# Two-stage set attention and SwiGLU on one core: order of the first stages, wait of GpSimd for VectorE's integer steps, 64-column unread products, new lists

## The chip, the cores and the metric

The kernel runs on one core of a Trainium2 chip. The metric is the device time of one launch in microseconds (us), the median of several runs. The engines of the core are TensorE (PE; its weight loads are shown as PEld), VectorE (DVE), ScalarE (ACT) and GpSimd (POOL); each works through its own instructions in the order in which the program issues them. Transfers are issued by the sync queue (SP).

## The reference

x has 4 batches of 12,416 rows of 128 channels, `inducing` 32 rows. Per batch there are two attentions without projections, then a gated feed-forward layer over all 49,664 rows with d_ff = 1,536:

```python
def mab(q, kv):
    s = scale * (q @ kv.transpose(0, 2, 1))
    s = s - s.max(-1, keepdims=True)
    a = np.exp(s)
    a /= a.sum(-1, keepdims=True) + 1e-09
    return a @ kv
h = mab(I, x)
x2 = mab(x, h)                                  # (B, N, C), then (B*N, C)
rms = np.sqrt(np.mean(x2 * x2, axis=-1, keepdims=True) + 1e-06)
xn = x2 / rms * rms_g
g = xn @ w_gate
out = (g / (1.0 + np.exp(-g)) * (xn @ w_val)) @ w_out
```

The three weight matrices reach the kernel as 64-bit floats.

## The kernel before, in words

**Algebra.** The rows of x2 are weights `a` (32 numbers a row) times h. The kernel normalizes `a` itself and multiplies it with `h @ w_gate` and `h @ w_val` ("stacks" `sg` and `sv`), so that a gate product has only the 32 weights in two halves (high and low part, each twice: 128 rows) as its moving side.

**Tiling.** A batch is cut into 7 sets of rows (`NS`), these into 25 units of up to 512 rows; with 12 column blocks of d_ff there are 4 x 25 x 12 = 1,200 blocks. Each has a gate product (`gate`, L709), SiLU (L719), a value product (`value`, L737), their multiply (`times_value`, L751) and the product with `w_out`. The last comes in three kinds, given by the list `sorts`: P is one plain 32-bit product (in two instructions, L807), S and D are three products in a faster 32-bit form (L795, L796, L807) of a high and a low part. S makes the parts with ACT (L764) and DVE (L770) and adds them with POOL (L815); D with ACT (L761, L783) and POOL (L777, L815).

**Order by hand.** The order of everything is written out in lists of letters. `ORDER` is that of the first stages (batch 0 up to its first two units), `program` that of the rest; each letter issues one step, and a "." in `program` takes the next number of `taken`, a step outside the blocks (attention of the next batch, norms, the other weights). `banks` and `BANKS` tell which of the 8 PSUM banks each product writes to, `workers`, `outputs`, `holders` and `picks` which buffer a step uses and which of the waiting blocks it takes.

**The first stages.** Names of `ORDER` that matter here, with s a set, k a part, i a weight matrix (0 gate, 1 value, 2 out) and c one of its three chunks of 512 columns or rows; a last letter A, V or G names the engine (ACT, DVE, POOL):

- `t`sk, `c`sk: PE turns four tiles of x (L934), a copy out of PSUM (L919 on ACT, L923 on DVE)
- `s`, `m`, `own`, `mB`, `nb`, `e`, `r`, `h`: scores of a set (PE, L316), their eviction with a maximum (DVE, L945), the maximum of a group of sets (L951, L959, L962), exponentials (ACT, L970), transpose (DVE, L354), sum with x (PE, L978). `ls`, `share`, `shared`, `tl`, `spl`, `rl`, `fr`, `hs`, `th` bring the groups together, `hT` copies the turned h (ACT, L919), `hg` scales it.
- `p`ic, `u`ic, `g`ic, `l`ic: a weight's 64-bit word taken apart on DVE: exponent (`power`, L231), upper mantissa (`upper`, L244), sign (`sign`, L253), lower mantissa (`lower`, L259). These are the integer steps. `P` and `U` turn two of them into numbers (L209, L211, L213); `j`ic multiplies the two on POOL (`join`, L265); `q` stores the chunk and fetches the next.
- `sc`, `T`, `rm`, `sub`, `ex`, `ta`, `sq`, `zm`, `sm`, `mm`, `rt`, `ap`, `tb`, `hi`, `lo`, for parts 0, 1, 2 of set 0: scores against h (PE, L1025), transpose (DVE, L1028), row maximum (DVE, L1032) and its subtraction (L1036), exponential (ACT, L1041), transpose (DVE, L1045), product with the Gram matrix of h (PE, L1049), its multiply and sum (DVE, L1053, L1058), clamp (L1062), power -1/2 (POOL, L1066), multiply (L1070), transpose (DVE, L1073), high and low part (L1078, L1084).
- `st`i, `stc`i, `low`i: the first third of a stack (PE, L479; ACT, L482; DVE, L486). It needs `j`i0.
- `sdh`, `sdl`, `sdm`, `cpa`, `cpb` for units 0 and 1: selection products that spread the halves over 128 rows (PE, L1088) and their copies to the gate product's moving side.
- `w`n: n products of the identity with itself into bank 5, which nobody reads (`warm`, L158); 7 stand at the start of the kernel as well. Each is a 32-bit product in two instructions with a weight load each.
- `silu`: a first SiLU, with its table load (ACT, L1107).

In the `program` part a step of the kinds `power`, `upper`, `sign`, `lower` makes the next POOL instruction wait for it; this is a dependency made by hand, with the reason "no two at the shared port". `ORDER` is gone through without it (`for name in ORDER.split(): do[name]()`).

Of the kernel before, what the change touches and what calls it, by code (L numbers as in the profile page):

```python
# [18 lines left out]
P = 128  # L19
# [4 lines left out]
def kernel(  # L24
# [10 lines left out]
    nc = tc.nc  # L35
# [119 lines left out]
    def warm(n):  # L155
        ps = pall[:, 5, :]
        for _ in range(n):
            nc.tensor.matmul(ps[:, 0:P], ident[:], ident[:], start=True, stop=True)  # L158
# [113 lines left out]
    turns, works, outs, factors = [], [], [], []  # L272

# [600 lines left out]
    for s in (1, 2, 0, *range(3, NS)):  # L874
# [20 lines left out]
        sdm0 silu tb1 hi1 cpb0A p01 cpa0V lo1V P01A w1 sdh1 sdm1 sdl1 cpb1A cpa1A u01 U01V  # L895
# [6 lines left out]
    def first():  # L902
# [217 lines left out]
        for n in range(1, 40):  # L1120
            do[f"w{n}"] = lambda n=n: warm(n)
# [124 lines left out]
    def seams():  # L1246
# [13 lines left out]
        5672340156372450721456701425140571240715420745127450172407512510752317052317024537032407263742746043267304234073  # L1260
        4270327053127305127031251512450126401526140526041245143624532757364735263456735745146517507654107641754055172457
        3571725742135724130725412354615267526471260541072467043764162106714625014725437240732413072103271403716207365127
        6351726513267136364716376471630714306217420761405726450145102614264350264032520754302434750324102475146506267467
        0526470357620165073126507261576507610576501463154634165462526531246534127651675042607456270452706534253761374623
        4726314672312470612764125714257162517462714751467104360146703476014721367306327652062763765230176501201327041270
        2731047230276346734267432643572453670524605246104561462105640216412354362514516521467562317546230152304624254302
        4675204375230170412032731243710421013641263416536253421632451637167457614164501765124705140512521054314523045301
        2754207356047235275204352407310723420473407624073062753046705435637306350160576132751037501347531740537415074316
# [290 lines left out]
```

## Time and profile before

| | |
|---|---|
| median of 3 runs | 1476.39 us (1476.35 to 1476.93) |
| profiled execution | 1473.84 us, of it the span 1472.1 |
| PE, DVE, ACT, POOL busy | 99%, 97%, 89%, 93% of the span |
| mean granted TensorE clock | 0.999 |
| x of batch 0 | 6.4 MB, in five loads of 1 MB and some smaller ones |

The span goes from the first to the last instruction. A row of the timeline or of the costliest groups has the engine, the source line, the operation, what it writes and reads, shapes, the count, and in brackets the idle time before it with what ended it. In a timeline a row begins with start and duration in us, and instructions of one kind in a row are merged (x2, x3). In the chain of waits a row has start, duration and the engine and line that the end depended on. A matmul's end is modelled.

### The profile page before, as it was taken

The numbers are of one execution on the slowest core, as the hardware profiler recorded it, in microseconds if no ns is written. First come the engines' busy times: TensorE is split into PE (matmuls) and PEld (weight loads), VectorE is DVE, ScalarE is ACT, GpSimd is POOL, SyncE is SP. The second block draws the span as 40 slices with busy tenths as digits, with TensorE's granted clock in tenths as the row PEclk, the third lists the DMA queues.
The fourth block names the chain that finished last, engine by engine and source line by source line (L and its number), as shares of the span: only waits on it lengthen the run. The fifth ranks groups of instructions, "written<-read, shape, count | busy, mean of one in ns | idle before, by whom it ended". The sixth has DMA issues, their size and how long they took to land.

```text
span 1472.1 us, 26044 instructions
## 1 busy us (share of the span) xinstructions
PE 1462.6 (99%) x7303; PEld 1105.9 (75%) x7303; DVE 1427.8 (97%) x2483; ACT 1305.7 (89%) x2604; POOL 1374.5 (93%) x1212
## 2 busy tenths in 40 slices
PE   9999999999999999999999999999999999999998
PEld 7566777867777777786777777787777777777787
DVE  7999999999999999999999999999999999999998
ACT  5798899889998889998989898998998899989997
POOL 1499998999999999899999999899999999999998
PEclk9999999999999999999999999999999999999999
DMA  7754323557434131455655212263322112122122
GB/s 282 148 102 101 68 42 75 114 128 137 84 66 87 29 70 39 104 122 107 127 89 108 51 36 47 50 130 94 67 57 47 33 37 44 37 40 40 38 41 35
DMA packets 391904, 116.02 MB, mean 79 GB/s; under 512 B 365648, under 2 KB 371280, under 8 KB 389200
## 3 DMA queue, kind: packets, MB, share of 16 engines
q1 hardware_dynamic: 391168, 114.28, 37.7%
q8 instruction: 58, 0.95, 0.3%
q14 instruction: 86, 0.70, 0.2%
q10 hardware_dynamic: 592, 0.08, 0.0%
HBM read 53.95 MB, written 27.00 MB: 55 GB/s over the span
## 4 chain that ended last, share of the span: by engine, by line
PE 96%; DVE 1%; DMA 1%; issue 0%; SPq 0%; POOL 0%; ACT 0%; DVEq 0%
PE gv L807 32%; PE gv L709 17%; PE gv L737 17%; PE gv L795 12%; PE gv L796 12%; PE gv L316 3%; PE gv L369 1%; DMA xn<-in_x_dram 1%; PE gv L563 1%; PE gv L457 0%; PE gv L978 0%; SPq L104 0%; DVE o L259 0%; DVE u L751 0%; PE gv L934 0%
## 5 line engine op out<-in xcount | busy, mean ns | idle before, releaser
L719 ACT ACTIVATE silu<-gv 128x512 f32<-128x512 f32 (+2 forms) x1200 | 675.0, 591 | 81.1 <-PE gv L709 64.6
L815 POOL TENSOR_TENSOR xn<-xn,xn 128x512 fp32r<-128x512 f32 (+2 forms) x489 | 604.8, 1252 | 15.2 <-PE gv L796 10.3
L709 PE MATMUL gv<-a,sg 128*128 128x512 f32 (+2 forms) x1188 | 481.6, 432 | 0.0
L737 PE MATMUL gv<-a,sv 128*128 128x512 f32 (+2 forms) x1188 | 449.7, 411 | 0.0
L751 DVE TENSOR_TENSOR gv<-silu,gv 128x512 f32<-128x512 f32 (+2 forms) x653 | 429.0, 676 | 7.5 <-ACT silu L719 3.6
L764 ACT ACTIVATE xn<-gv 128x512 fp32r<-128x512 f32 (+1 forms) x630 | 368.7, 597 | 31.9 <-DVE gv L751 26.0
L751 DVE TENSOR_TENSOR u<-silu,gv 128x512 f32<-128x512 f32 (+2 forms) x547 | 347.6, 653 | 7.5 <-PE gv L737 3.9
L807 PE MATMUL gv<-u,wo 128*128 128x512 f32 (+2 forms) x718 | 352.1, 575 | 0.2 <-POOL wo L265 0.2
L770 DVE SCALAR_TENSOR_TENSOR xn<-xn,gv 128x512 fp32r<-128x512 f32 (+2 forms) x508 | 332.0, 664 | 7.1 <-ACT xn L764 4.8
L709 PEld LDWEIGHTS gv<-a,sg 128*128 128x128 f32 x1188 | 224.4, 190 | 100.0 <-issue 30.5
L737 PEld LDWEIGHTS gv<-a,sv 128*128 128x128 f32 x1188 | 223.8, 189 | 90.3 <-issue 21.1
L815 POOL TENSOR_TENSOR xn<-xn 128x512 fp32r<-128x512 f32 (+2 forms) x185 | 232.5, 1260 | 7.5 <-PE gv L796 4.7
L777 POOL TENSOR_TENSOR xn<-u,xn 128x512 fp32r<-128x512 f32 (+2 forms) x166 | 204.5, 1237 | 12.7 <-ACT xn L761 11.4
L815 POOL TENSOR_TENSOR u<-xn,u 128x512 fp32r<-128x512 f32 (+1 forms) x143 | 180.0, 1267 | 0.8 <-PE gv L796 0.7
L795 PE MATMUL gv<-xn,xn 128*128 128x512 f32 (+2 forms) x447 | 169.7, 380 | 0.0
L807 PEld LDWEIGHTS gv<-u,wo 128*128 128x128 f32 x718 | 133.8, 190 | 26.9 <-issue 9.5
L807 PE MATMUL gv<-xn,xn 128*128 128x512 f32 (+2 forms) x372 | 139.5, 386 | 0.0
L796 PE MATMUL gv<-xn,xn 128*128 128x512 f32 (+2 forms) x372 | 139.1, 374 | 0.0
L795 PE MATMUL gv<-xn,more 128*128 128x512 f32 (+2 forms) x341 | 131.3, 385 | 0.0
L761 ACT ACTIVATE xn<-u 128x512 fp32r<-128x512 f32 (+2 forms) x187 | 115.6, 619 | 9.6 <-DVE u L751 8.1
L783 ACT ACTIVATE xn<-xn 128x512 fp32r<-128x512 f32 (+2 forms) x187 | 116.3, 628 | 7.0 <-POOL xn L777 5.8
L807 PE MATMUL gv<-xn,more 128*128 128x512 f32 (+2 forms) x286 | 110.8, 392 | 0.0
(235 smaller groups left out, 1840.5 us busy)
## 6 DMA issues: line engine op xcount, KB each, us to landing
out_dram<-o SPq DMA_DIRECT2D x320, 64.0 KB, 2.0
xT<-in_x_dram SPq DMA_DIRECT2D x60, 256.0 KB, 4.4
xn<-in_x_dram SPq DMA_DIRECT2D x60, 256.0 KB, 5.1
a<-hi SPq DMA_DIRECT2D x152, 64.0 KB, 2.0
a<-lo SPq DMA_DIRECT2D x152, 64.0 KB, 2.0
xn<-in_x_dram SPq DMA_DIRECT2D x5, 1024.0 KB, 9.3
xn<-w SPq DMA_DIRECT2D x18, 256.0 KB, 4.1
out_dram<-o SPq DMA_DIRECT2D x64, 60.0 KB, 2.0
```

What stands on the lines that cost most here:

```text
L709: nc.tensor.matmul(g[:, 0:T], stacks[b][0][:, ts(j, P)], halves_in_turn(one["a"][:, 0:T]), start=True, stop=True)
L719: nc.scalar.activation(sl[:, 0:T], gates.pop(n)[:, 0:T], AF.Silu)
L737: nc.tensor.matmul(v[:, 0:T], stacks[b][1][:, ts(j, P)], halves_in_turn(one["a"][:, 0:T]), start=True, stop=True)
L751: nc.vector.tensor_tensor(out=to, in0=sl[:, 0:T], in1=v[:, 0:T], op=ALU.mult)
L764: nc.scalar.activation(hi, t["u"], AF.Copy, scale=-(1.0 - 2.0 ** -13) * 2.0 ** -12)
L770: nc.vector.scalar_tensor_tensor(out=t["lo"], in0=t["hi"].bitcast(F32), scalar=4096.0, in1=t["u"], op0=ALU.mult, op1=ALU.add)
L777: nc.gpsimd.tensor_tensor(out=t["lo"], in0=t["u"], in1=t["hi"].bitcast(F32), op=ALU.subtract)
L783: nc.scalar.activation(t["hi"], t["hi"].bitcast(F32), AF.Copy, scale=-(2.0 ** -12))
L795: nc.tensor.matmul(to, weight_of(0, j), halves_in_turn(t["hi"]), start=not one["q"], stop=False)
L796: nc.tensor.matmul(to, weight_of(1, j), halves_in_turn(t["lo"]), start=False, stop=last)
L807: nc.tensor.matmul(to.rearrange("p (n h) -> p h n", h=2) if step2 else to, lhsT, rhs, start=one["left"] == NJ, stop=one["left"] == 1)
L815: nc.gpsimd.tensor_tensor(out=t["lo"], in0=t["hi"].bitcast(F32), in1=t["lo"].bitcast(F32), op=ALU.add)
```

## The change

Four things change.

1. The dependency by hand moves into a function `in_turn` that both `ORDER` and `program` use. In `ORDER` the locking steps are p, u, g, l, the number steps P and U where DVE does them, and `frV`. A lock is kept in one list, `held`, and taken by the next step that issues a POOL instruction.
2. `warm` takes a number of columns; the products of `ORDER` have 64 columns, those at the start keep 128. `ORDER` before has w11 w1 w2 w1 w2 w4 w1 (22 products), after w9 w3 w2 w2 w4 w1 w1 w14 w2 w2 (40).
3. `ORDER`, `BANKS` and `OUTPUTS` are new. The steps are the same but for the unread products and for the engine of some: c20, c23, c33, c32, c30 and cpa0 go from DVE to ACT, c01, c02, c43 and U11 from ACT to DVE, sub0 and ap1 from POOL to DVE, sub2, lo0 and lo1 from DVE to POOL.
4. `banks`, `workers`, `holders`, `sorts`, `picks`, `program` and `taken` are new. The steps numbered in `taken` are the same 879. `sorts` before has 359 P, 653 S and 188 D, after 360 P, 651 S and 189 D.

```diff
-    def warm(n):
+    def warm(n, columns=P):
         ps = pall[:, 5, :]
         for _ in range(n):
-            nc.tensor.matmul(ps[:, 0:P], ident[:], ident[:], start=True, stop=True)
+            nc.tensor.matmul(ps[:, 0:columns], ident[:], ident[:, 0:columns], start=True, stop=True)
...
+    held = []
+
+    def in_turn(step, args, lock):
+        made = len(nc.cur_bb.bb.instructions)
+        step(*args)
+        new = nc.cur_bb.bb.instructions[made:]
+        if lock:
+            held[:] = new[-1:]
+        elif held and new and new[-1].engine == mybir.EngineType.Pool:
+            tc.add_manual_dep(new[0], held.pop().name, mybir.DependencyInfo(mybir.DependencyClass.Sync, mybir.DependencyReason.DATA),
+                              reason="no two at the shared port")
...
-        0123410234012340123401234012304132041320413024301
+        0123401234031240312403214031240312430124301243120
...
-    OUTPUTS = "01010"
+    OUTPUTS = "01110"
     ORDER = """
-        open w11 t13 t11 t12 t10 c11A w1 t21 c12A t23 c13V c10V t20 c21A s1 c20V t01 c23V c01A m1 t00 c00A t22 t03 t02
-        c22A s2 c02A c03V s0 m2 t31 m0 own0 t33 c31V c33V t43 mB0 nb0 t30 c30V c43A e2 t32 c32V t40 c40V t41 t53 e1 c41A
-        r2 t42 r1 t60 c53A p00 u00 e0 t51 c60A c42A ls0 t52 r0 t50 s3 c51A s6 c50A s4 c52A p10 P10A m3 P00A s5 m6 p20
-        P20A h0 m4 m5 own1 mB1 own2 mB2 g00 U00A nb1 l00 e3 nb2 u20 h1 h2 r3 h3 e5 r5 e4 j00 e6 least r4 ls1 h5 ls2
-        share shared tl r6 g10 spl rl U20A h4 q00 hs0A frA th0 u10 hs1A h6 l20 g20 U10A l10 hs2A th1 th2 hTA w2 sc0 p11
-        hgA sqh gc T0 rm0 sc1 j20 T1 sub0G ex0 rm1 sub1G sc2 T2 ta0 ex1 u11 ta1 st0 sq0 zm0 stc0 U11A q20 j10 q10 P11A
-        sm0 mm0V w1 sq1 rt0 rm2 zm1 sub2V sm1 ex2 mm1V w2 st1 stc1 ap0V tb0 hi0 low0 w4 sdh0 rt1 lo0V low1 sdl0 ap1G
-        sdm0 silu tb1 hi1 cpb0A p01 cpa0V lo1V P01A w1 sdh1 sdm1 sdl1 cpb1A cpa1A u01 U01V
+        open w9 t12 c12A t13 t10 t11 c11A c13V w3 t22 c22A c10V t21 c21A t20 t23 s1 m1 t02 c02V t03 c03V t01 c01V c20A
+        t00 c23A s2 m2 c00A s0 t33 m0 t32 c33A c32A t30 c30A own0 mB0 nb0 e0 e1 t31 c31V t43 c43V r1 t41 t40 c40V t42
+        c41A t50 c42A c50A r0 s3 m3 s4 e2 p00 m4 ls0 t53 c53A t60 c60A t52 t51 own1 r2 c52A c51A p10 mB1 nb1 s6 u10 u00
+        h0 m6 e3 r3 s5 m5 h1 e4 U00A ls1 own2 P00A l00 w2 mB2 nb2 U10A e5 g00 h3 j00 h2 r4 h4 e6 least ls2 r5 share
+        shared r6 tl p20 p01 hs0A spl P10A hs1A h5 rl frA th0 P20A u20 g10 q00 l10 U20A l20 h6 hs2A g20 th1 w2 th2 hTA
+        w4 sc0 T0 hgA P01A sc1 T1 rm0 sqh j20 gc sc2 rm1 sub1G sub0V T2 ex0 ta0 ex1 ta1 st0 rm2 j10 w1 sq0 stc0 zm0 sm0
+        sub2G mm0V sq1 ex2 zm1 rt0 sm1 mm1V low0 ap0V tb0 silu hi0 rt1 ap1V w1 st1 stc1 tb1 lo0G hi1 w14 sdh0 q20 w2
+        sdl0 p11 sdm0 lo1G cpa0A sdh1 low1 cpb0A P11A w2 sdm1 u01 u11 q10 cpb1A U01V sdl1 cpa1A U11V
     """
...
         for n in range(1, 40):
-            do[f"w{n}"] = lambda n=n: warm(n)
+            do[f"w{n}"] = lambda n=n: warm(n, P // 2)
...
+        locks = {f"{key}{i}{c}{by}" for i, c in chunks for key, by in (*zip("pugl", ("",) * 4), ("P", "V"), ("U", "V"))} | {"frV"}
         for name in ORDER.split():
-            do[name]()
+            in_turn(do[name], (), name in locks)
...
-    held = None
     alone = {id(one[name]) for one in weight.values() for name in ("power", "upper", "sign", "lower")}
     for name in "".join(program.split()):
-        made = len(nc.cur_bb.bb.instructions)
         step, args = micros[int(next(taken))] if name == "." else (do[name], ())
-        step(*args)
-        one = nc.cur_bb.bb.instructions[-1]
-        if id(step) in alone:
-            held = one
-        elif held is not None and one.engine == mybir.EngineType.Pool and len(nc.cur_bb.bb.instructions) > made:
-            tc.add_manual_dep(one, held.name, mybir.DependencyInfo(mybir.DependencyClass.Sync, mybir.DependencyReason.DATA),
-                              reason="no two at the shared port")
-            held = None
+        in_turn(step, args, id(step) in alone)
```

More of the change, by code (lines that the diff above doesn't have):

```diff
@@ new lines @@
+        6720354672506235761365107217150271357321453214532352634576345236537465027362570165013567015670310567046102471604
+        2176412670427106257642347206247056240567401256421632630246034614326405316403640167034673146750361752631452641734
+        1234126470321470231540235140213450213542153641527571624764652416732643624321406340130261704631063573167436147563
+        1456347236425302653420635246305435276452163471645364751730657460346543625046250365412305273402173124707301723416
+        3042630423145235023512401573421734620424147160761265402174627340763714672143641732471612754121027450724150724517
@@ new lines @@
+        0235146532416541265342531206170213271671016031267262634126132545463162163574617206301671467134063076104531075243
+        7054705315043704315761074265076060146567160174615734173245323724705432573025304720562307306020716037263702413764
+        3051764564170417654670215421407145317437014530745301675317231562132561236573172351751752170152145741035210214320
+        1420414034201632046203516051630513065731065731754031712305270153207520123457215325726721562153671236571437615745
+        3674530657340634153104321041540352032103205360523605236036720675203167531607506745675160764576214174621376134261
@@ L1285 @@
+        4657041257014630576
     """
     workers = """
-        20120201201201022012102210210211212012100120120102012012020120120
+        20120120120101012012012120120120102201212102102102012012021021021
     """
@@ L1313 @@
+        sqjpabrenkdlomjcipshfqnkrmjlopgaskdmjqrpnlosbkmejqrlphsofkcijmnqrlapsgojmkdrlnqebfpohjsimkracgdbnlehi
     """
     sorts = """
[L1315 to L1317 removed]
@@ new lines @@
+        AAAAAAAAAAAAAAAAAAAAAAAAACBAAAAAAAAABAAAAAAABAAAAAABAAAAAAAAAAABAAAABAAAAAAAAAAAABAAAAAAAAABAAAAAAACAAABABAAAAAA
+        AAAAABAAAAAAAAAABAABAAABAAAABAAAAAAAAAAAAAAAAAAAAAAAAAAAAAAACAABAAAAAAAAAAAAAABAAAABAAAAAAAAAAAAAAAABAAAAAAAAAAA
+        AAAAAAAAAABAAAAAAABAAABAAAAAAAAAAAAAAAAAAAAAAAAAAAAAAAAAAAAAAAAABAAAAAAAAABAAAAAAAAAAAAAAAAAAAAAAAAABAAAAAAAAABA
+        AAAAABAAAAAAAAAAAAAAABAAAAAAAAAAAABAAAAAAAAAAAAAAAAAAAAAAAAAACABAAABAAAAAABAABAAAAAAAAAAAAAAAAAAAAAAAAAAAAABAABB
+        AABAAAAAAAABAAAAAAAAAAAAABAAAAAABBABAAABAABAA
```

377 lines of the change are left out of this document (180 added, 197 removed), and 60 rows, old and new, of the table taken.

## The prediction

> **What bounds the kernel now.** I read the page first, then the busy time of each engine by stretches, then the chain of waits, then the first 50 us instruction by instruction.
>
> ```profile
> span 1472.1 us, 26044 instructions
> PE 1462.6 (99%) x7303; PEld 1105.9 (75%) x7303; DVE 1427.8 (97%) x2483; ACT 1305.7 (89%) x2604; POOL 1374.5 (93%) x1212
> ```
>
> TensorE (PE) is busy for all but 9.5 us of the span. The stretches (length, busy time of PE, PEld, DVE, ACT and POOL with counts, granted clock, DMA share, GB/s) say where those are not:
>
> ```profile
> 200.00:400.00 200.00, 200.00 (x1061) 150.66 (x1059) 193.71 (x323) 181.25 (x364) 188.88 (x173) 1.00 0.51 102
> 1200.00:1400.00 200.00, 200.00 (x845) 157.00 (x844) 199.17 (x331) 181.88 (x351) 198.27 (x161) 1.00 0.21 40
> ```
>
> In the steady part PE is busy in all of 200 us, while VectorE (DVE) still has 6.3 us and 0.8 us to spare. A busy PE is modelled, so I test it on the chain, which gives each product's share:
>
> ```profile
> 71.98 0.86 PE gv L807 x2
> 72.84 0.43 PE gv L737 x2
> ```
>
> A gate or value product costs 0.22 us, the two halves of a plain output product 0.86, a split output product three times 0.22. The lists hold 1,200 gates, 1,200 values, 359 plain and 841 split blocks. In the stretch from 1200, which holds little else, 845 products in 200 us are 0.237 us each, which leaves no room for waits beside the plain ones' longer time. So from about 50 us on PE's own work sets the end, and whatever the lists do there can only lose. What can be won lies ahead of that, and behind PE's last product.
>
> ```profile
> 4.10 15.92 DMA xn<-in_x_dram
> ...
> 1467.65 0.45 DVE o L854
> ```
>
> The first of these rows of the chain says that up to 20 us everything waits for x; no order of the engines changes that. The second is the last transpose: 4 us behind it belong to the store. What is left to the change is 20 to 50 us.
>
> ```profile
> 21.70 0.43 DVE L231 TENSOR_SCALAR we<-sc 128x512 int32<-128x512 int32 x1
> ...
> 31.39 0.41 DVE L244 TENSOR_SCALAR o<-sc 128x512 int32<-128x512 int32 x1
> 31.71 0.68 DVE L259 SCALAR_TENSOR_TENSOR o<-sc,o 128x512 f32<-128x512 uint32 x1
> 33.07 1.27 POOL L265 TENSOR_TENSOR wo<-o,we 128x512 f32<-128x512 f32 x1 [3.80 <-DVE we L253]
> 33.10 1.79 DVE L259 SCALAR_TENSOR_TENSOR o<-sc,o 128x512 f32<-128x512 uint32 x1
> 33.90 0.27 ACT L919 COPY hT<-gv 128x128 f32<-128x128 f32 x1 [0.58 <-PE gv L999]
> 34.24 0.43 PE L1025 MATMUL gv<-xT,hT 128*32 128x128 f32 x8
> 34.81 0.41 DVE L231 TENSOR_SCALAR we<-sv 128x512 int32<-128x512 int32 x1
> 35.15 0.30 DVE L1028 STREAM_TRANSPOSE sc<-gv 128x128 f32<-128x128 f32 x1
> 35.92 0.87 POOL L1036 TENSOR_TENSOR sc<-sc,mx 128x128 f32<-128x128 f32 x2 [1.58 <-ACT gram L424]
> 36.35 0.31 ACT L1041 ACTIVATE sc<-sc 128x128 f32<-128x128 f32 x1 [0.52 <-POOL sc L1036]
> 36.75 1.27 POOL L265 TENSOR_TENSOR silu<-o,we 128x512 f32<-128x512 f32 x1
> 36.93 1.37 DVE L244 TENSOR_SCALAR o<-sv 128x512 int32<-128x512 int32 x1
> 38.22 0.30 DVE L1045 STREAM_TRANSPOSE eT<-sc 128x128 f32<-128x128 f32 x1
> 38.45 0.25 DVE L1053 TENSOR_TENSOR eT<-gv,eT 128x128 f32<-128x128 f32 x1
> 39.08 0.17 DVE L1062 TENSOR_SCALAR ms<-ms 128x4 f32<-128x4 f32 x1
> 39.33 1.04 POOL L1066 TENSOR_TENSOR rs<-ms,mhalf 128x4 f32<-128x4 f32 x1 [1.31 <-DVE ms L1062]
> 39.35 1.02 PE L479 MATMUL gv<-silu,hg 128*128 128x512 f32 x2
> 39.68 0.41 DVE L1036 TENSOR_TENSOR sc<-sc,mx 128x256 f32<-128x256 f32 x1
> 40.43 0.28 DVE L1070 TENSOR_TENSOR sc<-sc,rs 128x128 f32<-128x128 f32 x1
> 41.09 0.69 DVE L486 TENSOR_TENSOR sg<-gv,sg 64x512 fp32r<-64x512 f32 x1
> 41.41 1.28 ACT L1107 ACT_TABLE_LOAD   x1
> 41.45 0.33 PE L1088 MATMUL gv<-hi,u 128*128 128x128 f32 x1 [0.18 <-ACT hi L1078]
> 45.05 1.00 PE L709 MATMUL gv<-a,sg 128*128 128x512 f32 x2
> ```
>
> Two things are to be seen in this timeline. First, two integer steps of DVE are far too long, and each starts beside a GpSimd (POOL) multiply: L259 takes 1.79 us at 33.10 (0.68 at 31.71), L244 takes 1.37 at 36.93 (0.41 at 31.39). Both end 0.28 to 0.55 us after the POOL step does: they stood still for 1.1 and 0.96 us. Second, the last row is the first gate product; it comes 25 us after the last of x.
>
> ```profile
> 45.00:46.00 1.00, 1.00 (x5) 0.82 (x5) 1.00 (x4) 0.96 (x3) 0.00 (x0) 0.60 1.17 190
> 46.00:47.00 1.00, 1.00 (x4) 0.81 (x3) 1.00 (x3) 0.74 (x2) 0.00 (x0) 0.50 0.21 32
> 47.00:48.00 1.00, 1.00 (x4) 0.69 (x3) 1.00 (x3) 0.64 (x2) 0.13 (x1) 0.50 0.00 0
> 48.00:49.00 1.00, 1.00 (x6) 0.17 (x8) 1.00 (x2) 1.00 (x3) 0.52 (x2) 0.69 0.00 0
> 49.00:50.00 1.00, 1.00 (x16) 0.25 (x8) 0.32 (x2) 1.00 (x4) 0.84 (x1) 1.00 0.00 0
> ```
>
> Right then the granted clock is 0.60, 0.50, 0.50 and 0.69 of full speed: 0.40 + 0.50 + 0.50 + 0.31 = 1.71 us of PE's work lost while PE was the bound.
>
> **The change, part by part.** *The added wait.* Three products (j00, j20, j10) are POOL's integer joins. In the new order the last locking step ahead of j00 is g00, and ahead of j20 it is g20; both are operands of the join anyway, so the wait adds nothing there. j10 and the rest have no lock left before them; lo1G waits for p11, and the first POOL step of the main part for U11V; behind lo1G on POOL stands only that main part, which PE reaches later. So the dependency itself costs about 0 (bounds: nothing below, one step of 0.41 above). What does act is the order: no integer step follows j00, j20 or j10 closely any more. u11 and p11 go behind tb1, and l10 ahead of j20. That takes both stalls out, 1.1 and 0.96 us.
>
> *How far that reaches, stage by stage.* T0 (L1028) waited for DVE until 35.15: behind the stalled l10 and behind p11 (34.81). In the new order p01 comes in for p11 (the same operation, 0.41), and p00 starts at 21.70 in both if it waits for its weights. DVE is thus early by the stall of 1.1 us. But hT is copied at 33.90 by ScalarE (ACT), whose queue has at least as much ahead of it as before, so T0 can start no sooner than the end of sc0, 34.24 + 0.43 = 34.7: a gain of 0.45. Then T1 stands ahead of the first maximum, and rm1 ahead of sub0V: two steps of 0.3 give it back. sub0V ends near 36.2, and the exponential starts at 36.25 against 36.35: a gain of 0.1. Next, ta1 no longer waits for u11 until 38.22; but rm2 (0.41) now stands there. zm0 starts near 37.65 instead of 38.45, mm0V at 38.2 instead of 39.08, and rt0 at 38.5 instead of 39.33: 0.85 us gained. Behind it low0 (0.69, the row at 41.09) has moved ahead of ap0V: ap0V starts at 39.9 rather than 39.5, against 40.43: 0.5 us gained. The next, hi0, is 0.5 us early, at about 40.6 to 40.9. The table load of 1.28 us (41.41) now stands ahead of hi0 on ACT; behind ex2 it runs from 39.1 to 40.6 with the small SiLU, so it costs nothing as long as ex2 isn't later than that.
>
> A price that I can only bound is that of mm1V beside rt0 on POOL: it may stand still as L244 did (up to 1.04 us), or not. The nearest row is the subtraction at 39.68, which ran wholly beside the same rt0 and took 0.41; by it the cost is 0, which I take, with up to 0.6 us above it (the rest is cover that low0 has to spare). The Trainium skill, "SBUF — State Buffer" in its section on the shared port pair, has a stricter rule: a VectorE step with two SBUF inputs and a GpSimd step that reads SBUF exclude one another for a whole instruction. By that rule mm1V would wait for rt0's end, 0.6 us more at the first gate, and the time would be 1474.9 (an estimate). The stalls at 33.10 and 36.93 agree with it, the 0.41 at 39.68 doesn't.
>
> *The unread products.* Their number goes from 22 to 40 beside the first 7, each with half the columns.
>
> ```profile
> 26.38 0.52 PEld L959 LDWEIGHTS gv<-owns,fold 128*128 128x128 f32 x4 [0.36 <-DVE owns L951]
> 40.21 0.86 PEld L158 LDWEIGHTS gv<-ident 128*128 128x128 f32 x7 [0.24 <-issue]
> ```
>
> Four weight loads for products of 8 columns take 0.52 us, so (0.52 - 0.19) / 3 = 0.11 us from one to the next (0.19 is one alone); seven for unread products of 128 columns (0.86 - 0.19) / 6 = 0.11. The load sets the pace, not the columns: an unread product (two passes) is worth 0.22 us, with 64 columns as with 128. That is 40 x 0.22 = 8.8 us instead of 4.8. Most lies in waits. w14 is the one that doesn't: 14 x 0.22 = 3.1 us behind st1 and ahead of sdh0. st1 needs j10, which ends near 37.65 (sub1G till 36.4, then 1.27), and takes 1.02: w14 runs from 38.7 to 41.85, where hi0 is there at 40.9. So sdh0 starts at 41.85 against 41.45: the 0.5 us are gone and 0.4 lost. At the other bound, half the price for half the columns, w14 ends at 40.3 and is hidden. From the start of sdh0 to the first gate the old kernel took 3.6 us, though the 16 selection products between are only 16 x 0.11 = 1.8: PE waited there for tb1, which stood behind low0 and low1. In the new order tb1 is early, lo0G on POOL runs under the first w2, and two w2 cost 0.44 each. I count 1.8 + 0.9 = 2.7 us: a first gate at 44.55 instead of 45.05, **-0.5 us** (from -1.4 with w14 at half price to +1.0 with mm1V stalled and a later p00).
>
> *The clock.* PE is now occupied from st1 through the selection products nearly without a wait, which is what the stretch from 38 to 45 lacked. I take it that the dip is gone: **-1.7 us** (bounds 0 and -1.7).
>
> *The lists.* Plain blocks 359 to 360, S blocks 653 to 651, D blocks 188 to 189: one product more of 0.86 for one of 0.65 is 0.2 us, and the block that lost is wider or narrower than the one that won, so 0 to 0.2; 0.1 taken. S blocks use DVE twice, so DVE loses 1.3 us, hidden behind PE. What the new order does to PE in the steady part isn't in this trace: not below 0, since PE has no idle time to give; above, any wait counts in full. I take 0. The last steps behind PE are the same ones.
>
> Sum: -0.5 - 1.7 + 0.1 = -2.1 us. The profiled execution took 1473.8 (1472.1 and 1.7 around it), the median is 1476.4; the difference is carried over to the median: **1474.3 us**.
>
> **The rivals.** *The clock dips all the same.* For it: half the columns give the array half the work per load, and the dip began behind products that were also spaced by loads. Against: PE is occupied far more. The time is 1476.4 - 0.5 + 0.1 = 1476.0. The Trainium skill, "TensorE: Matmul & The Clock Gate", Part 1, has activity judged in a free-running window of 3.4 us, and the row of clocks agrees in length (0.60, 0.50, 0.50, 0.69 are 3.4 us at half speed); by that rule the dip may also come or go from run to run.
>
> *The whole start gains.* w14 lies in the wait (half price) and ACT has hT ready when DVE is, 0.65 us before the 34.7 above: -1.4 - 0.65 - 1.7, so 1472.7. For it: DVE's lead of 1.1; against: the two rows of weight loads.
>
> *Slower: PE waits in the steady part.*
>
> ```profile
> L751 DVE TENSOR_TENSOR gv<-silu,gv 128x512 f32<-128x512 f32 (+2 forms) x653 | 429.0, 676 | 7.5 <-ACT silu L719 3.6
> ```
>
> DVE has 0.8 us in 200 free late in the kernel. If the new lists put the multiply of one block in each of the 100 units so late that PE finds no free bank, each time 0.08 us (an eighth of L751's 0.68), that is 8 us: 1476.4 - 2.1 + 8 = 1482. It decides from 0.05 us a unit on, where it passes +0.2%. For it: every bank, holder and pick is new, and no row shows them; against: the old lists, of the same kind and the same counts, show no wait at all.
>
> *The change doesn't do what it says.* The wait adds no constraint of its own, as shown; this is in the forecast.
>
> **How the numbers follow.** The forecast, -2.1 us, 0.40; the dip remains 0.19; the whole start gains 0.21; slower in the steady part 0.20. What a measurement of this kernel tells from no change is about 0.2%, 2.95 us: faster means below 1473.4. That takes the third case (0.21) and a quarter of the forecast's, 0.31 in all; slower 0.20; the rest 0.49. Range: the forecast's own is 1473.2 to 1475.4 (bounds of the start); it has to reach 1471.8 for the third case with its bounds, and upward into the slow one until 2 in 10 are left: 1479.8.
>
> **What would show it.** Right: no DVE integer step over 0.8 us in 20 to 50; weight loads of w14 0.11 us apart and its end after hi0; a first gate at 44.0 to 45.0; clock 1.00 in 40 to 50; PE busy 200.00 in the steady stretches. Wrong: half the spacing in w14; a clock below 1 after the first gate; PE idle after 60 us, with DVE or a bank as the releaser; a first gate after 46.

## The result: 0.24% slower, and the profile after

The changed kernel takes 1478.81 us (median of 15 runs, 1475.11 to 1480.45), the kernel before beside it 1474.89 (15 runs, 1472.79 to 1476.93): a ratio of 1.0024, 95% interval 1.0016 to 1.0032. A little slower, then, where 1474.3 was forecast, a gain of 2.1. The profiled execution took 1478.81, with a span of 1476.9.

In the page and the windows of the changed kernel (columns as before; every main line stands 11 further down, so the gate is L720, the value L748, the plain output product L818) two things are new:

```profile
span 1476.9 us, 26147 instructions
PE 1467.8 (99%) x7338; PEld 1111.7 (75%) x7338; DVE 1423.9 (96%) x2478; ACT 1303.2 (88%) x2606; POOL 1374.9 (93%) x1213
...
L720 PE MATMUL gv<-a,sg 128*128 128x512 f32 (+2 forms) x1188 | 484.7, 434 | 1.1 <-ACT xn L772 1.1
L748 PE MATMUL gv<-a,sv 128*128 128x512 f32 (+2 forms) x1188 | 445.9, 408 | 1.4 <-DMA a<-lo 1.0
```

```profile
40.00:50.00 10.00, 10.00 (x76) 8.75 (x78) 9.41 (x26) 7.27 (x18) 4.70 (x6) 1.00 0.67 154
110.00:120.00 10.00, 8.85 (x35) 6.31 (x35) 9.30 (x17) 8.68 (x17) 8.62 (x8) 1.00 0.70 131
200.00:400.00 200.00, 199.04 (x1060) 150.64 (x1059) 192.03 (x320) 178.68 (x362) 190.86 (x175) 1.00 0.49 98
1200.00:1400.00 200.00, 200.00 (x851) 158.00 (x850) 199.69 (x333) 182.14 (x352) 198.75 (x162) 1.00 0.20 39
```

The dip of the clock between 45 and 49 us is gone (1.00 in 40 to 50). But PE, which never waited after 64 us, now waits once in 110 to 120 (8.85 busy of 10) and once in 200 to 400 (199.04 of 200).

The larger loss is ahead of all that. The timeline of PE's weight loads shows it, first after, then before:

```profile
5.07 3.92 PEld L158 LDWEIGHTS gv<-ident 128*128 128x128 f32 x18
8.76 3.43 PEld L945 LDWEIGHTS gv<-ident,xn 128*128 128x128 f32 x16
```

```profile
4.65 2.53 PEld L158 LDWEIGHTS gv<-ident 128*128 128x128 f32 x22
7.10 1.78 PEld L934 LDWEIGHTS gv<-ident,xn 128*128 128x128 f32 x16
```

The 16 loads of the first transposes of x need (1.78 - 0.19) / 15 = 0.11 us each before, and 0.22 after; so do the 18 loads of w9. PE ran at half speed until 12 to 13 us. The granted clock can't say this: it shows 1.00 until the trace's first record of a change. That first record, "clock now full", is at 4.2 us before and at 12.7 after. From 4.8 us to the first gate all of PE's work is on the path; from the chain of waits after (start, duration, what):

```profile
5.14 4.03 PE gv L158 x18
9.18 3.41 PE gv L945 x16
...
42.43 3.07 PE gv L158 x28
```

From 4.8 to 49 us the chain holds PE and nothing else, the unread products (L158) among it. Before, it was the arrival of x until 20 us.

Stage by stage (the kernel with 128-column products is the first experiment):

| start of, us | before | after | after, 128 columns |
|---|---|---|---|
| clock full (first record) | 4.2 | 12.7 | 4.8 |
| hT copied (ACT) | 33.90 | 37.30 | 33.51 |
| T0 (DVE) | 35.15 | 38.52 | 34.79 |
| rt0 (POOL) | 39.33 | 42.09 | 38.35 |
| first sdh product (PE) | 41.45 | 45.31 | 41.58 |
| first gate (PE) | 45.05 | 48.02 | 44.30 |
| span less first gate | 1427.0 | 1428.9 | 1427.6 |

After minus before is 3.0 us at the first gate, and 1.9 behind it although the dip is gone.

### The profile page after: what moved, and what is told of

Read it like the earlier page. It is cut to its first block, busy times and chain, and to the rows that moved or that the text cites. A ratio compares the mean times of both kernels' runs of the same rounds, so it can differ in the third digit from the quotient of the medians.

```text
span 1476.9 us, 26147 instructions
## 1 busy us (share of the span) xinstructions
PE 1467.8 (99%) x7338; PEld 1111.7 (75%) x7338; DVE 1423.9 (96%) x2478; ACT 1303.2 (88%) x2606; POOL 1374.9 (93%) x1213
## 4 chain that ended last, share of the span: by engine, by line
PE 98%; DVE 1%; ACT 1%; DMA 0%; issue 0%; SPq 0%; DVEq 0%
PE gv L818 32%; PE gv L748 17%; PE gv L720 17%; PE gv L806 12%; PE gv L807 12%; PE gv L327 3%; PE gv L380 1%; PE gv L945 1%; PE gv L158 1%; PE gv L574 1%; PE gv L989 0%; PE gv L468 0%; DMA ind<-in_inducing_dram 0%; PE gv L490 0%; DVE u L762 0%; ACT silu L730 0%
## 5 line engine op out<-in xcount | busy, mean ns | idle before, releaser
L720 PE MATMUL gv<-a,sg 128*128 128x512 f32 (+2 forms) x1188 | 484.7, 434 | 1.1 <-ACT xn L772 1.1
L748 PE MATMUL gv<-a,sv 128*128 128x512 f32 (+2 forms) x1188 | 445.9, 408 | 1.4 <-DMA a<-lo 1.0
L775 ACT ACTIVATE xn<-gv 128x512 fp32r<-128x512 f32 (+2 forms) x620 | 364.5, 599 | 35.6 <-DVE gv L762 28.1
L818 PE MATMUL gv<-u,wo 128*128 128x512 f32 (+2 forms) x720 | 353.7, 575 | 0.1
L781 DVE SCALAR_TENSOR_TENSOR xn<-xn,gv 128x512 fp32r<-128x512 f32 (+2 forms) x513 | 336.5, 666 | 6.9 <-ACT xn L775 4.7
L720 PEld LDWEIGHTS gv<-a,sg 128*128 128x128 f32 x1188 | 223.6, 189 | 98.4 <-issue 33.8
L748 PEld LDWEIGHTS gv<-a,sv 128*128 128x128 f32 x1188 | 223.2, 189 | 91.7 <-issue 24.9
L826 POOL TENSOR_TENSOR xn<-xn 128x512 fp32r<-128x512 f32 (+2 forms) x192 | 238.7, 1249 | 16.6 <-PE gv L807 13.5
L806 PE MATMUL gv<-xn,xn 128*128 128x512 f32 (+2 forms) x459 | 177.5, 387 | 0.0
L826 POOL TENSOR_TENSOR u<-xn,u 128x512 fp32r<-128x512 f32 (+2 forms) x123 | 155.1, 1268 | 2.5 <-PE gv L807 2.4
L818 PEld LDWEIGHTS gv<-u,wo 128*128 128x128 f32 x720 | 134.0, 190 | 27.2 <-issue 9.2
L818 PE MATMUL gv<-xn,xn 128*128 128x512 f32 (+1 forms) x388 | 145.8, 385 | 0.0
L807 PE MATMUL gv<-xn,xn 128*128 128x512 f32 (+1 forms) x388 | 145.5, 375 | 0.0
L806 PE MATMUL gv<-xn,more 128*128 128x512 f32 (+2 forms) x324 | 122.6, 378 | 0.0
L806 PEld LDWEIGHTS gv<-xn,xn 128*128 128x128 f32 x459 | 86.9, 189 | 19.2 <-issue 4.9
```

The costliest lines, as they stand in the source:

```text
L720: nc.tensor.matmul(g[:, 0:T], stacks[b][0][:, ts(j, P)], halves_in_turn(one["a"][:, 0:T]), start=True, stop=True)
L748: nc.tensor.matmul(v[:, 0:T], stacks[b][1][:, ts(j, P)], halves_in_turn(one["a"][:, 0:T]), start=True, stop=True)
L775: nc.scalar.activation(hi, t["u"], AF.Copy, scale=-(1.0 - 2.0 ** -13) * 2.0 ** -12)
L781: nc.vector.scalar_tensor_tensor(out=t["lo"], in0=t["hi"].bitcast(F32), scalar=4096.0, in1=t["u"], op0=ALU.mult, op1=ALU.add)
L806: nc.tensor.matmul(to, weight_of(0, j), halves_in_turn(t["hi"]), start=not one["q"], stop=False)
L807: nc.tensor.matmul(to, weight_of(1, j), halves_in_turn(t["lo"]), start=False, stop=last)
```

## The experiments

Each gave a profile and 11 or 12 runs; the kernel before ran 33 to 35 times beside each group of four, with medians of 1473.85 (e1 to e4), 1473.04 (e5, e6, e8, e9) and 1474.01 (e7, e10 to e12). Each group ran on a chip of its own. In all three groups its runs lie in three heaps: 1472.4 to 1473.1, 1473.8 to 1474.9 and 1475.6 to 1476.5 (51, 22 and 30 runs; medians 1472.74, 1474.04 and 1475.93). "Opening" is the first record of full clock.

### Is it the 64 columns? e1, e4, e3 and e9

e1, all products of `ORDER` at 128 columns; e4, only the first two groups:

```diff
-            do[f"w{n}"] = lambda n=n: warm(n, P // 2)
+            do[f"w{n}"] = lambda n=n: warm(n)
```

```diff
-            do[f"w{n}"] = lambda n=n: warm(n, P // 2)
+            do[f"w{n}"] = lambda n=n: warm(n, P if n in (9, 3) else P // 2)
```

> The changed kernel with 128 columns in all unread products of ORDER. Clock theory (at 64 columns the products of the first 9 us don't open TensorE's clock, which was half until 12.7 us in the changed kernel's profile and until 4.2 us in the old one's): the first gate comes 2 to 3.5 us earlier than the 48.0 us of the changed kernel, weight loads between 5 and 9 us stand 0.11 us apart, and the time is 2 to 3.5 us under the changed kernel's. Rival, the order itself (w14 and the later scores): nothing changes, since the weight load sets the pace; first gate at 48, time as the changed kernel's. Rival, the new main lists: the same, no change.

> The changed kernel with 128 columns in w9 and w3 alone, the products ahead of 13 us; all later ones keep 64. Clock theory: as fast as with 128 everywhere within 0.5 us, because only the opening of the clock matters. If 64 columns also hurt later (a dip near the first gate), it stays 1 to 2 us behind that kernel. Rivals: no change against the changed kernel.

e1: 1474.33 us, ratio 1.0004 (0.9995 to 1.0012), opening at 4.8, first gate at 44.30. e4: 1475.08, ratio 1.0008 (0.9999 to 1.0016), opening at 6.9, first gate at 45.21. So widening the 12 products of w9 and w3 is enough to bring the first gate from 48.0 to 45.2 us.

e3 is the old kernel with its 22 products at 64 columns:

```diff
-            nc.tensor.matmul(ps[:, 0:P], ident[:], ident[:], start=True, stop=True)
+            nc.tensor.matmul(ps[:, 0:columns], ident[:], ident[:, 0:columns], start=True, stop=True)
...
-            do[f"w{n}"] = lambda n=n: warm(n)
+            do[f"w{n}"] = lambda n=n: warm(n, P // 2)
```

> The old kernel with 64 columns in the unread products of ORDER, nothing else. Clock theory: the clock opens later than 7 us in most executions, first gate 2 to 3 us later than 45.05, time 1.5 to 3 us over the old kernel's, and the dip after the first gate stays. Rivals (order, main lists): the same time as the old kernel within 0.5 us.

e3: 1474.93, ratio 1.0007 (0.9995 to 1.0020), but in heaps: five runs at 1472.5 to 1472.8, two at 1474.9 to 1475.3, four at 1477.5 to 1478.9. The profile, of the run at 1474.93, has the opening at 5.9 and 6.8 us of half clock from 43.4 on. The mean granted clock of the other runs is 0.999 or 1.000 in the first five, 0.999 in the one at 1477.5 and 0.997 in the three above it: these three have stretches of half clock in them, and whether any run of e3 opened late is not shown. So the late opening is no constant price; e9, the changed kernel once more, settles that:

> The changed kernel itself, beside these. Theory (a late clock from 64 columns): half-speed weight loads up to 12 us, first gate at 47 to 48.5, the same two waits near 119 and 371 us, ratio to the kernel before 1.0016 to 1.0032 as in its first measurement. Rival (what was seen in the one profile was chance): clock open by 5 to 7 us, first gate at 44.3 to 45.5, ratio 1.000 to 1.001.

e9: 1477.49, ratio 1.0017 (1.0007 to 1.0027), in two heaps: five runs at 1473.8 to 1474.4, seven at 1476.9 to 1478.9. The profiled execution was one of the first heap. Its weight loads:

```profile
4.86 2.48 PEld L158 LDWEIGHTS gv<-ident 128*128 128x128 f32 x18
7.21 1.79 PEld L945 LDWEIGHTS gv<-ident,xn 128*128 128x128 f32 x16
```

Opening at 5.7, transposes at full speed, first gate at 44.57, with the very program that had 12.7 and 48.02. Of the four profiles with the new order and 64 columns, the three of long runs opened late (after 12.7, e8 12.8, e2 10.8) and the one of a short run early (e9). Both theories of this run were half right: the late clock is real, and it is a lottery. In the first measurement 13 of 15 runs drew the long heap, here 7 of 12. With full-width first products (e1, e4, e5 to e7, e10 to e12) no profile opened later than 7.4 us, and no run was above 1476.6.

### Are the new lists of the steady part to blame? e2, e5 and e8

e2 is the changed kernel's start followed by the old lists (`banks`, `workers`, `holders`, `sorts`, `picks`, `program`, `taken`); e5 the same with 128 columns:

```diff
-        .gg.vs.vg.sgvs.g.......gm.msp.msv..s....gg.m.p..svp..v..v.g....mp.ms.mps..vg..psmp...g.vsvvmp.....v.gm...msp...v
...
+        ..ggvs..v.gsgg.sg......m..msp.s....vvvmpmsv.m.pmvg..s...g..vm.s..mp......p....p...vg..g..s.ps....vm.pmg.p..s...g
...
```

> The changed kernel's first stages (ORDER, 64 columns, wait) with the old lists for the rest. Main-list theory (the new lists make TensorE wait in the steady part, 2.5 us in the waits of the changed kernel's profile): 2 to 3.5 us faster than the changed kernel, from the first gate to the end as in the old kernel less its clock dip (1425.5 us). Clock theory alone: no faster than the changed kernel, first gate at 47 to 48.

> The changed kernel's start, all of its unread products at 128 columns, followed by the old lists of the steady part. Theory (the new order of the start is good, its 64-column products open the clock late, and the new lists of the steady part cost time by themselves): first gate at 44.3 us as in the run of the changed kernel with 128 columns, no stretch at half clock after it, span less first gate 1425.5 to 1427.1 (1427.0 before less the dip's 1.6, and the 1427.1 of the 64-column start with the old lists), so a span of 1469.8 to 1471.4 and a run of 1471.5 to 1473.1 on a chip where the kernel before is at 1473.85: a ratio of 0.998 to 0.9995. Rival (the new start hands over badly whatever lists follow, by VectorE's integer steps that it leaves undone): span less first gate 1427.6 or more, ratio 1.000 to 1.001, as with the new lists.

e2: 1475.82, ratio 1.0010 (1.0001 to 1.0019), heaps at 1472.6 to 1473.3 (four) and 1475.6 to 1477.1 (eight). e5: 1473.68, ratio 0.9996 (0.9987 to 1.0005), all runs between 1473.16 and 1474.42. The heaps of e2 lie 1.3 and 1.6 us below those of the changed kernel in e9 (medians 1472.96 and 1476.8 against 1474.29 and 1478.4). They ran on different chips; the lowest heaps of the kernel before, 1472.69 and 1472.95 there, differ by 0.3 in the same direction, which leaves 1.1 and 1.3. The ratios of e1 and e5 differ by 0.0008, 1.2 us. Span less first gate says the same without the clock's lottery: 1427.0 to 1427.1 with the old lists behind the new start (e2, e5, e10), 1427.6 to 1428.9 with the new ones (e1, e4, e7, e9 and after; mean 1428.3). So the new lists cost some 1.3 us. e5 was to reach a ratio of 0.998 to 0.9995; it ends 0.0001 short of that, at the upper edge of the 1425.5 to 1427.1 expected behind the gate. Against before without its dip (1427.0 - 1.6 = 1425.4) e5 loses 1.6 us behind the gate with the same lists: 0.5 by 100 us, another 1.0 in steps of 0.25 to 0.5 between 240 and 1140 us, where the list of PE's waits shows none; single products there start 0.3 to 0.4 us behind the one before instead of 0.22. The old start loses 0.9 of the 1.6 in the same way once its dip is gone (e12 below), so 0.7 at most is the new start's own. What these steps are stays open.

Why the lists cost time: the wait at 119 us after, with SyncE's queue ahead of it (start, duration, what is issued):

```profile
110.18 2.74 SPq L880 DMA_DIRECT2D out_dram<-o  x4
112.96 0.63 SPq L111 DMA_DIRECT2D xT<-in_x_dram  x1
113.69 2.06 SPq L658 DMA_DIRECT2D a<-hi  x1
...
117.07 0.58 SPq L658 DMA_DIRECT2D a<-lo  x1
```

```profile
119.26 0.67 PE L720 MATMUL gv<-a,sg 128*128 128x512 f32 x2 [1.15 <-ACT xn L772]
```

This gate is the first of a unit and reads `a`, whose four gathers are issued from 113.69 to 117.65, behind four stores. The gathers of `lo` there land 1.9 to 2.2 us after their issue, the last of the four at 119.06. The page names an ACT step as releaser; it ended at 119.16, so the times alone can't part the two, but in the trace PE's queue stands at its wait for the gathers from 117.28 to 119.09. e8 puts this group of stores, and another ahead of the wait at 371 us, behind the gathers:

```diff
-        svgrhpm.nm.svr..hpsm.gevlvhgmps.m.sq...vTq.vmpOm.gp.n..vh..dslp.Td.q..Orgsdpmsve.r.vhgmrvsqm.nvEpma.gdeg.vps.sgm
+        svgrhpm.nm.svr..hpsm.gevlvhgmps.m.sq...vTq.vmpOm.gp.n..vh..dslp.Td.q..rgsdpmsve.r.vhgmrvsqm.nvEpmaO.gdeg.vps.sgm
...
-        hrvFrsgqslvsvn.mgvqmsggdmepms.vsTdgghvmgsvOrmnphmsqslghvdrmgsvqeamvnspmhghdlvrsqleg.vmdsqvmErqh.mdgglsrvqsF.dvhv
+        hrvFrsgqslvsvn.mgvqmsggdmepms.vsTdgghvmgsvrmnphmsqslghvdrmgsvqeaOmvnspmhghdlvrsqleg.vmdsqvmErqh.mdgglsrvqsF.dvhv
```

> The changed kernel; in the steady part's order two groups of four stores of the output go behind the gathers that follow them on SyncE's queue: the group issued at 110.2 to 112.9 us, and the one at 364.1 to 366.8. Theory (the two waits of TensorE that the changed kernel has after 100 us, 1.1 us at the first gate of a unit at 119 and 1.0 us at a value product at 371, are gathers issued late because stores are ahead of them on the queue, 0.67 us each): both waits shrink below 0.3 us, TensorE is 200.0 busy in 200 to 400 us where only this lies, and the run falls by 1.5 to 2.1 against the changed kernel run beside it. Rival (the gathers wait for their data, or for the free rooms of DMA queue, not for the stores): the waits stay at 0.7 to 1.1, and the run within 0.5. Second rival: the wait goes, but an o buffer comes free late and TensorE or VectorE waits 2 us for it: no gain.

e8: 1475.49, ratio 1.0008 (0.9998 to 1.0017); its profile has the late clock too (12.8), so it compares with after directly:

```profile
110.95 1.44 SPq L658 DMA_DIRECT2D a<-hi  x1
112.49 0.55 SPq L658 DMA_DIRECT2D a<-lo  x1
113.09 0.58 SPq L658 DMA_DIRECT2D a<-hi  x1
113.72 0.58 SPq L658 DMA_DIRECT2D a<-lo  x1
114.40 2.62 SPq L880 DMA_DIRECT2D out_dram<-o  x4
```

The gathers go out 3 us sooner and both waits are gone (of PE's waits after 60 us none above 0.4 is left). Product for product PE is 0.70 us earlier than after behind the first place and 1.50 behind the second, but 0.4 are given back in small steps after 1150 us: span less first gate 1427.9 against 1428.9. The theory holds for the cause, and promised more than the 1.0 it gave. The medians, 1475.49 here and 1477.49 in e9 beside it, say more than that only by the lottery of the clock: e8 had six runs of twelve in its long heap, e9 seven. Heap for heap (medians 1473.96 and 1477.82 against 1474.29 and 1478.4) the gain is 0.3 and 0.6. In e9 only one such wait was there (0.9 at 115.5), in e1 0.4 and 0.3: how long they are depends on how the transfers fall.

### The added wait, and w14: e7 and e6

e7 is e1 without the added wait; e6 is e1 with w7 for w14:

```diff
-            in_turn(do[name], (), name in locks)
+            in_turn(do[name], (), False)
```

```diff
-        sub2G mm0V sq1 ex2 zm1 rt0 sm1 mm1V low0 ap0V tb0 silu hi0 rt1 ap1V w1 st1 stc1 tb1 lo0G hi1 w14 sdh0 q20 w2
+        sub2G mm0V sq1 ex2 zm1 rt0 sm1 mm1V low0 ap0V tb0 silu hi0 rt1 ap1V w1 st1 stc1 tb1 lo0G hi1 w7 sdh0 q20 w2
```

> The changed kernel with 128 columns and without the added wait of GpSimd for VectorE's integer steps in the start. Theory (the wait adds no constraint, the order alone keeps the two apart): the first gate within 0.15 us of 44.3 + 0.47 x (clock opening - 4.8), as in the runs with 128 columns and the wait; no VectorE step of L231, L244, L253 or L259's form (128x512, whole numbers) between 20 and 50 us longer than 0.85 us; the run within 0.5 of the kernel with the wait (ratio 1.0004). Rival (the wait does its work): one or more of these steps is 1.3 to 1.8 us long beside a GpSimd operation, the first gate 0.4 to 1.1 later, the ratio 1.0007 to 1.0012.

> The changed kernel with 128 columns, and 14 loads instead of 28 between the last sorting step and the first sdh product. Theory of the prediction (these products aren't hidden: the first sdh product stood at 41.58, 0.83 us after its hi was written at 40.75): it starts at 40.8, and the first gate comes 0.4 to 0.8 us sooner, at 43.5 to 43.9; if the clock stays at 1.00 in 40 to 50 us the run is 0.4 to 0.8 below the same kernel with 28 loads (1474.3 where the kernel before is at 1473.85). First rival: the products hold the clock; without half of them TensorE idles more than the clock allows, a dip of 3.4 us comes between 42 and 50 us and costs 1.6, so the run is 0.8 to 1.2 above. Second rival: the next lo products come no sooner, the first gate stays within 0.15 of 44.3.

e7: 1475.23, ratio 1.0003 (0.9994 to 1.0012). Opening at 6.9 and first gate at 45.26; 44.3 + 0.47 x 2.1 is 45.29. No integer step between 20 and 50 us is longer than 0.80 us. The wait does nothing here, the order does it all.

e6: 1474.66, ratio 1.0002 (0.9994 to 1.0011). Opening at 7.1, first gate at 44.63, which is 0.75 below 44.3 + 0.47 x 2.3 = 45.38, as the first theory had it, and no dip came. The time didn't follow; PE's timeline of e6 shows where it went:

```profile
48.81 1.10 PE L818 MATMUL gv<-u,wo 128*128 128x512 f32 x2 [0.83 <-DVE u L762]
```

The first plain product waits 0.83 us for VectorE, which has its integer steps to do at that time. What w14 held back at 41 us was going to wait at 49.

### Can the good parts be had alone? e10, e11 and e12

e10 is e5 with w4 for w9. e11 has w1 for w3 and w9 for w14 as well:

```diff
-        open w9 t12 c12A t13 t10 t11 c11A c13V w3 t22 c22A c10V t21 c21A t20 t23 s1 m1 t02 c02V t03 c03V t01 c01V c20A
+        open w4 t12 c12A t13 t10 t11 c11A c13V w1 t22 c22A c10V t21 c21A t20 t23 s1 m1 t02 c02V t03 c03V t01 c01V c20A
...
-        sub2G mm0V sq1 ex2 zm1 rt0 sm1 mm1V low0 ap0V tb0 silu hi0 rt1 ap1V w1 st1 stc1 tb1 lo0G hi1 w14 sdh0 q20 w2
+        sub2G mm0V sq1 ex2 zm1 rt0 sm1 mm1V low0 ap0V tb0 silu hi0 rt1 ap1V w1 st1 stc1 tb1 lo0G hi1 w9 sdh0 q20 w2
```

> The new start with 128 columns and the old lists (first gate 44.96 with the clock open at 6.2), with 8 unread loads instead of 18 ahead of the first transposes. Theory (TensorE is busy without a gap from 5 us to the first gate, so every unread product that it needn't wait with is on the path): the rows land at 5.7, the transposes start at 5.8 to 6.7 instead of 6.85 to 8.05, and the first gate comes 1.1 to 1.9 sooner than 44.3 + 0.47 x (opening - 4.8); the run 1.0 to 1.9 below the same start with 18 loads, ratio 0.9984 to 0.999. Rival (the later loads of x, which land from 8.2 to 20.4 us, set the pace): TensorE waits for a load between 8 and 20 us, the first gate stays within 0.3 of that line, ratio 0.9996. Second rival: fewer full columns in the first windows, the clock opens one window later (9 to 11 us) in some runs, which then are 2 to 3.5 longer.

> As the run with 8 loads ahead of the first transposes, with 2 instead of 6 unread loads ahead of the second group and 18 instead of 28 before the first sdh product. Theory (unread products on the path): another 0.4 + 0.7 off the first gate, which comes 2.0 to 2.7 sooner than 44.3 + 0.47 x (opening - 4.8); of the last 0.7 some 0.4 come back as a wait for VectorE after the gate (0.83 at 48.8 with 14 loads); the run 1.5 to 2.3 below the start with all of them. Rival (loads of x set the pace until 20 us, VectorE after 44): the first gate 0.7 sooner at most, the run within 0.4.

e10: 1472.15 us, ratio 0.9985 (0.9976 to 0.9994). e11: 1471.68, ratio 0.9982 (0.9973 to 0.9991), all its runs between 1471.44 and 1472.12: faster than both kernels, and still 1.0 below the lowest heap of the kernel before beside it (median 1472.69). First gates at 44.41 (opening 7.4) and 42.64 (opening 6.1), 1.1 and 2.3 below the line 44.3 + 0.47 x (opening - 4.8). From the chains of waits of e5 and of e11:

```profile
4.94 2.84 PE gv L158 x18
...
39.37 3.13 PE gv L158 x28
```

```profile
4.93 1.69 PE gv L158 x8
6.62 1.75 PE gv L945 x16
...
38.16 0.69 DVE sg L497
```

With ten loads fewer the transposes start 1.1 us sooner and nothing later takes it back; PE has no wait for x in either. In e11 the chain leaves PE for VectorE at 36.5: the unread products ahead of sdh0 are no longer on it.

e12 is the old kernel with 128-column products in three waits:

```diff
-        sm0 mm0V w1 sq1 rt0 rm2 zm1 sub2V sm1 ex2 mm1V w2 st1 stc1 ap0V tb0 hi0 low0 w4 sdh0 rt1 lo0V low1 sdl0 ap1G
-        sdm0 silu tb1 hi1 cpb0A p01 cpa0V lo1V P01A w1 sdh1 sdm1 sdl1 cpb1A cpa1A u01 U01V
+        sm0 mm0V w1 sq1 rt0 rm2 zm1 sub2V sm1 ex2 mm1V w2 st1 stc1 ap0V tb0 hi0 low0 w4 sdh0 w2 rt1 lo0V low1 sdl0 ap1G
+        sdm0 silu tb1 hi1 cpb0A p01 cpa0V lo1V P01A w2 sdh1 w1 sdm1 sdl1 cpb1A cpa1A u01 U01V
```

> The kernel before, with 8 more unread loads of 128 columns where TensorE waits between 41.6 and 44.5 us (4 behind the first sdh products, where it waited 0.41; 2 ahead of the second, 0.24; 2 ahead of its next, 0.20). Theory (the half clock of 45.2 to 48.6 comes of those idle stretches in the window before it, and is what the change saved): first gate at 45.05 to 45.2 when the clock opens at 4.2, no stretch at half clock after it, span less first gate 1425.4 to 1425.9 (1427.0 less 1.6), run 1.1 to 1.6 below the kernel before where that has one such stretch, and the cluster of its runs at 1475 to 1476.5 gone: ratio 0.999 to 0.9995. Rival (the clock falls by something else, or by an earlier window): the stretch stays, the run the same within 0.3.

e12: 1472.89, ratio 0.9988 (0.9980 to 0.9997), eleven runs between 1472.67 and 1473.33, one heap. First gate at 45.20 (0.15 later), span less first gate 1426.3 (0.4 above the expected range: at the gate all 1.6 of the dip are gained, 0.9 are given back in small steps at 60 to 66 and near 700 us). Its median is 0.15 above the lowest heap of the kernel before. The windows of e12 where the kernel before had 0.60, 0.50, 0.50 and 0.69:

```profile
45.00:46.00 1.00, 1.00 (x8) 0.92 (x7) 1.00 (x3) 0.94 (x3) 0.00 (x0) 1.00 1.14 176
46.00:47.00 1.00, 1.00 (x6) 0.66 (x4) 1.00 (x3) 1.00 (x3) 0.00 (x0) 1.00 0.72 108
47.00:48.00 1.00, 1.00 (x13) 0.33 (x16) 1.00 (x3) 1.00 (x3) 0.00 (x0) 1.00 0.06 10
48.00:49.00 1.00, 1.00 (x13) 0.15 (x5) 1.00 (x3) 0.46 (x2) 0.71 (x2) 1.00 0.00 0
```

So the dip comes from PE's waits between 41 and 45 us, and it is what spreads the times of the kernel before. Its three heaps lie 1.3 and another 1.9 us apart, about as none, one and two stretches of 3.4 us at half clock would (1.7 each, 0.0012 of the span in the mean clock). The mean granted clock of each run fits: 0.999 or 1.000 in the lowest heap, 0.998 or 0.999 in the middle one, 0.997 or 0.998 in the highest. Where the stretches lie is seen in one profile only, that of before at 1473.84, with one of them; none was taken of a run in the other heaps.

## Why the prediction was wrong

The direction was wrong: -2.1 us was forecast, +3.9 measured; the time itself, 1478.81, lies within the range only by luck, at its slow end, where another mechanism had put it.

**The step that failed first: "The clock".** It priced the clock as the dip alone, 0 to -1.7 us, and never asked when the clock opens. The rival "the clock dips all the same" had the right thought, that half the columns give the array half the work per load, but looked for it at 45 us, where it does no harm: with the clock once open, w14 at 64 columns held it at 1.00. At 5 us the same products keep it shut. The clock changes on a grid of 3.41 us: before, the dip of 3.41 us begins 40.96 us, twelve such steps, behind the opening; in e3 the dip of 6.83, two steps, begins eleven steps (37.55) behind it. Steps back from 12.7 end at 9.3 and 5.9: after, the stretch between these two, full of loads with 64 columns, left the clock at half; the next, with the transposes' 128 columns, opened it. In e9 the stretch that ended at 5.7 was enough, in e3 (64 columns too) that at 5.9, and in after that at 5.9 wasn't, so the share of full-width products that decides lies close to what w9 leaves over; I have not measured that share. The Trainium skill, "TensorE: Matmul & The Clock Gate", Part 1, says that what is issued in the first 3.4 us or so runs cold (at half speed) and everything after at full speed, whatever the number of products. This trace doesn't agree: PE worked from 1.34 us on and was cold until 12.7, and by e4 the columns of the products count too.

Its price: each us of later opening moves the first gate by 0.47 (44.30 at 4.8, 48.02 at 12.7; e2, e4, e5, e7 and e9 lie within 0.2 of that line). At half speed it could be 0.50 at most. From 4.2 to 12.7 that is 4.0 us. The two heaps of e9 are 4.1 apart, which is not this price alone: from its opening at 5.7 to 12.7 the line gives 3.3, the first gates of the two profiles (44.57 and 48.02) are 3.45 apart, and the rest lies behind the gate (1427.9 against 1428.9, with one wait less).

**The step that failed second: "What the new order does to PE in the steady part ... I take 0."** It cost about 1.3 us on average and 1.9 in the profile of after. Of that 1.0 went in e8 with the single waits behind SyncE's queue, which the step did not look at; the other 0.9 stays open (1427.9 against the 1427.0 of the old lists, with no wait above 0.4). The slow rival feared the multiply in every unit, which did not come. The stretch behind the gate, not a term of the sum, gave back another 1.6 with the old lists; 0.9 of that the old start gives back too (e12).

**A premise that failed:** "up to 20 us everything waits for x; no order of the engines changes that." From 5 us to the first gate PE is busy without a gap in the changed kernel, w9 and w3 included; e10 and e11 are 1.6 and 2.1 us below e5 (by the ratios), by less filling and not by another order. "Most lies in waits" was wrong for the same reason.

**The base:** the forecast was carried to a median of 1476.39, three runs that all lay in the highest heap, though the profiled execution lay in the middle one. Fifteen runs give 1474.89.

**What held.** With the clock open early (the 128-column start) the order does what was worked out: T0 at 34.79 (34.7 in the text), rt0 at 38.35 (38.5), hi0 at 40.45 (40.6 to 40.9), sdh0 at 41.58 (41.85), the first gate at 44.30 (44.55). That is -0.75 against before, or about -1.0 at the same opening, for -0.5 forecast. Both stalls are gone, too: the longest integer step of after between 20 and 50 us takes 0.80 us. mm1V did not stand still beside rt0: its row in e1's timeline of VectorE,

```profile
38.84 0.17 DVE L1073 TENSOR_SCALAR ms<-ms 128x4 f32<-128x4 f32 x1
38.35 2.02 POOL L1077 TENSOR_TENSOR rs<-ms,mhalf 128x4 f32<-128x4 f32 x2 [0.31 <-DVE ms L1073]
```

is 0.17 us long wholly beside the power on POOL (second row). It has one input in SBUF (`ms`), as has the L244 that stalled at 36.93 before, while the rule that the prediction quotes is for steps with two; so neither row is a test of that rule, and the 1474.9 doesn't follow from it. The subtraction with two inputs (0.41 at 39.68) is. The loads of w14 are 0.11 us apart with 64 columns; this timeline row of after has 28 of its passes:

```profile
42.27 3.23 PE L158 MATMUL gv<-ident 128*128 128x64 f32 x28
```

The wait costs nothing (e7), and the dip went, worth 1.6.

The sum for the two profiled spans, 1472.1 and 1476.9: order -1.0, late opening +4.0, dip -1.6, new lists +1.9 (1428.9 against the 1427.0 of e5), given back behind the gate +1.6; together +4.9, and +4.8 measured. That the sum closes shows little: the terms up to the gate and those behind it are differences of the same profiles.

## What to carry to other kernels

A product that nobody reads is free only where TensorE really waits: look for PE in the chain of waits before calling a stretch bound by a load. If such products are there to open the clock, give them their full width until it is open, as w9 and w3 needed it here, and the price of one opening missed shows in the spacing of the weight loads, not in the granted clock. And where a kernel's runs lie in heaps, find out what each heap is before carrying a profile's sum to a median.

## What the runs showed that was not expected

- The same program opened the clock at 5.7 us in one execution and at 12.7 in another, worth 3.45 us at the first gate.
- 64-column products kept an open clock open and didn't open it. In e2, whose clock opened at 10.8, the grid's stretch from 41.5 to 44.9 held 3.1 us of them (28 passes until 44.3, others from 44.6), and the clock stayed at 1.00; after, the stretch from 5.9 to 9.3 held 3.3 us of them, and it stayed at half.
- Moving stores behind gathers on one queue took out 2 us of waits, and only 1.0 came through: small steps of 0.15 to 0.25 us, without a wait that the trace names, appear later and differ between profiles.
